# Linear-memory attention and a two-matrix feed-forward on one core: K and V in tiles of their own with fewer transfers, kept weights and first queries in larger packets, and three numbers of the schedule

## The chip, the cores and the metric

The kernel runs on one core of a Trainium2 chip. The metric is device time in microseconds (us) of one execution; lower is better. Before the change the median of three runs is 808.64 us (807.6 to 809.51).

## The reference

```python
a = phi - np.max(phi, axis=2, keepdims=True)      # phi: 8 batches, 8 heads, 576 tokens, 32 memories
a = np.exp(a)
a = a / (np.sum(a, axis=2, keepdims=True) + 1e-09)
k_m = np.einsum('bhsm,bhsd->bhmd', a, k)          # k, v, q: 8, 8, 576, 64
v_m = np.einsum('bhsm,bhsd->bhmd', a, v)
scores = scale * np.matmul(q, k_m.transpose(0, 1, 3, 2))
scores = scores - np.max(scores, axis=-1, keepdims=True)
attn = np.exp(scores)
attn = attn / (np.sum(attn, axis=-1, keepdims=True) + 1e-09)
x = np.matmul(attn, v_m)                          # then put as 4608 tokens by 512
h = x @ w_in                                      # w_in 512 x 2048
r = np.maximum(h, 0.0)
g = r * r
out = g @ w_out                                   # w_out 2048 x 512
```

The weights arrive as 64-bit floating-point numbers, and the kernel decodes them itself; the rest is 32 bits wide.

## The kernel before, in words

**Work.** Batches are handled in pairs. For each batch and each half `hh` of its heads (four heads), `memory(b, hh)` loads `phi`, K and V, takes the exponential and sums over the tokens with matmuls into the PSUM tile `pkv`: one pass for the sums of the exponential (`sums`, L465 to L471), one for K and V together (`mm`, L452). `scores(b, hh)` loads Q, transposes it on VectorE (L595), multiplies it with the K memory on TensorE (`psc`, L600) and transposes back (L604); a softmax follows. Batches 0 and 1 use `first_attention` instead, which transposes Q on TensorE (`pq`) and has its own score matmuls (`psc`, L662).

The attention output is never formed. `vw_alone` and `vw_step` multiply the V memory with a slice of `w_in` into `pvw` (L542, L562), so that `mm1(g)` goes from attention weights (`ath`, `atl`) straight to the hidden layer `h` (L766). Numbers are kept as a high and a low part, so a product is three matmuls. A step g is one batch and one block of 128 hidden units, 128 steps in all. After `h` come a relu into `r` (L770 on ScalarE or L771 on VectorE), the square's high part `gh` (L772, ScalarE), the full square (L774 or L775) and its low part `glo` (L776). `mm2(g)` adds these with `w_out` into four banks `acc` (L796, L797 from `gh`, L799 from `glo`). The 64 tokens left over beyond 512 are collected for two batches and done in `accl` (L822).

**Weights.** `decode` turns 512 KB of raw weights into a high and a low part with nine or so operations on VectorE and ScalarE, 32 times in all, ahead of the steps that use them. The decoded slices of `w_in` are written to two DRAM tensors, `w_in_hi` and `w_in_lo`, from the POOL queue (L390), and read again for each further pair of batches by `wi_again` on the SP queue (L395), two transfers of 256 KB each time.

**Order.** Nothing waits in program order as written. Each piece of work is recorded with a planned duration for each engine that can do it, what it reads and what it writes, and `Plan.order` lays all of it out by a model of the engines and the transfers; the kernel's instructions are then issued in that order. So numbers in the code that only describe durations move instructions. On the chip every engine's queue is in order, SP's queue of transfers too: a transfer that waits for a buffer holds those behind it. Buffers are tags: the tile `q` has one buffer, so Q of a batch's second half is loaded after the transposes (L595) of the first half; K and V of the next half batch are loaded after the matmuls L452 of the one before.

Of the kernel before, what the change touches and what calls it, by code (L numbers as in the profile page):

```python
# [19 lines left out]
P = 128  # L20
# [35 lines left out]
class Plan:  # L56
# [59 lines left out]
    def order(self):  # L116
# [30 lines left out]
        while len(out) < len(self.ops):  # L147
# [81 lines left out]
def tile_attention_moe(  # L229
# [54 lines left out]
    rate = {128: 100, 256: 220, 512: 288, 1024: 300, 2048: 312, 4096: 325, 4608: 325}  # L284
# [8 lines left out]
    def vec(ways, fn, r, w, **more):  # L293
        return op(ways, fn, r=r, w=w, **more)
# [27 lines left out]
    w_in_parts = []  # L322
    for x in ("hi", "lo"):
        t = dram.tile([DM, FF], F32, name=f"w_in_{x}")
        w_in_parts.append(plan.buf(f"w_in_{x}", lambda _, t=t: t))
# [3 lines left out]
    def wi_rows(x, s, hh):  # L329

        return w_in_parts[x]()[2 * hh * P:(2 * hh + 2) * P, s * SL:(s + 1) * SL].rearrange("(c p) f -> p c f", p=P)

    def decode(kind, j, h, room):

        rb, wb = (st([P, 2 * ND], U32, tag, name, 2 if tag == "KV" else 1) for tag, name in zip(room, ("raw", "work")))
# [52 lines left out]
        if kind == "wi":  # L388
            for x in (0, 1):
                dma(lambda d, x=x: d(wi_rows(x, j, h), t()[:, x].bitcast(F32)), [(2048 * P, 1024)], r=[(t, (h, x))], w=[(w_in_parts[x], (j, h))], eng="POOL", lead=True)  # L390

    def wi_again(n, s, hh):
        t = wi[n, s, 1, hh] = st([P, 2, 2, SL], F32R, "wi", f"wi{n}_{s}_{hh}", 3)
        for x in (0, 1):
            dma(lambda d, x=x: d(t()[:, x].bitcast(F32), wi_rows(x, s, hh)), [(2048 * P, 1024)], issue=440, r=[(w_in_parts[x], (s, hh))], w=[(t, (hh, x))], lead=True)  # L395
# [22 lines left out]
    def memory(b, hh, where=None):  # L418
# [550 lines left out]
```

## Time and profile before

| | |
|---|---|
| median of 3 runs | 808.64 us (807.6, 808.64, 809.51) |
| the profiled execution, its own time | 806.47 us |
| its span (first to last instruction) | 804.7 us, so 1.77 us lie around it |
| TensorE busy in the span | 774.5 us, 96% |
| VectorE, ScalarE, GpSimd busy | 561.7, 374.4, 64.7 us |
| bytes moved | 101.05 MB in 99,777 packets |

The profile names engines PE (TensorE matmuls), PEld (its weight loads), DVE (VectorE), ACT (ScalarE), POOL (GpSimd) and SP (the queue that issues most transfers). A row of a list in order of time has the start, the duration, engine, line, operation, what is written from what, and in brackets the idle time of the engine before it with what ended it. Matmuls overlap, so one that is listed with 0.39 us can be followed 0.23 us later by the next.

### The profile page before, as it was taken

How to read it: one execution, taken by the hardware profiler on the slowest of the kernel's cores; microseconds unless marked ns; L12 is line 12 of the kernel's file. 1: busy time of each engine (PE TensorE's matmuls, PEld its weight loads, DVE VectorE, ACT ScalarE, POOL GpSimd, SP SyncE). 2: the span in 40 equal slices, each digit the busy share in tenths (PEclk: the TensorE clock that was granted, in tenths of full speed). 3: DMA queues.
4: the chain of work that ended last, by engine and by line, in shares of the span. 5: the costliest groups of instructions: out<-in, count | busy, mean ns of one | idle time of the engine just before them, and what ended most of it. 6: DMA issues, size and time to landing. Idle time of an engine off the chain costs nothing.

```text
span 804.7 us, 13313 instructions
## 1 busy us (share of the span) xinstructions
PE 774.5 (96%) x4926; PEld 654.2 (81%) x4926; DVE 561.7 (70%) x1241; ACT 374.4 (47%) x871; POOL 64.7 (8%) x103
## 2 busy tenths in 40 slices
PE   4899999999999999999999999999999999999997
PEld 2677988888878888888887888788887888888885
DVE  4798867976669666966878566875779566775442
ACT  2667767865443454533343454443324345443220
POOL 4113112320101000010000100010000100000000
PEclk9999999999999999999999999999999999999999
DMA  7999865786645433321464522510524433101002
GB/s 229 278 314 285 234 176 170 217 226 178 186 118 160 121 106 105 81 50 29 128 173 122 130 95 91 138 30 25 147 63 119 128 113 99 37 7 47 1 0 66
DMA packets 99777, 101.05 MB, mean 126 GB/s; under 512 B 32320, under 2 KB 85568, under 8 KB 99712
## 3 DMA queue, kind: packets, MB, share of 16 engines
q1 hardware_dynamic: 89152, 81.42, 34.8%
q0 software_dynamic: 10464, 18.65, 8.9%
q8 instruction: 39, 0.64, 0.3%
q14 instruction: 26, 0.21, 0.1%
q10 hardware_dynamic: 96, 0.13, 0.1%
HBM read 79.17 MB, written 17.83 MB: 121 GB/s over the span
## 4 chain that ended last, share of the span: by engine, by line
PE 68%; DVE 13%; DMA 7%; issue 5%; ACT 4%; SPq 3%; POOL 1%; ACTq 0%; DVEq 0%; POOLq 0%
PE h L766 19%; PE acc L796 12%; PE acc L799 11%; PE acc L797 11%; DMA q<-in_q_dram 5%; PE accl L822 4%; DVE vw L571 3%; PE pvw L562 3%; PE pkv L452 2%; ACT vw L282 2%; ACT gh L772 1%; PE psc L600 1%; DVE qT L595 1%; DVE r L771 1%; DVE glo L776 1%
## 5 line engine op out<-in xcount | busy, mean ns | idle before, releaser
L796 PE MATMUL acc<-wo,gh 128*128 128x512 f32 x512 | 207.2, 405 | 3.9 <-ACT gh L772 3.9
L766 PE MATMUL h<-ath,vw 128*128 128x320 f32 (+1 forms) x1024 | 209.7, 299 | 0.1
L797 PE MATMUL acc<-wo,gh 128*128 128x512 f32 x512 | 201.5, 394 | 0.0
L766 PEld LDWEIGHTS h<-ath,vw 128*128 128x128 f32 x1024 | 169.0, 188 | 14.8 <-DVE r L771 0.9
L772 ACT ACTIVATE gh<-r 128x512 fp32r<-128x512 f32 x128 | 81.0, 633 | 194.1 <-DVE r L771 187.0
L799 PE MATMUL acc<-wo,glo 128*128 128x512 f32 x512 | 164.6, 406 | 0.7 <-DVE glo L776 0.5
L282 ACT CAST vw<-pvw 64x256 fp32r<-64x256 f32 (+1 forms) x224 | 84.2, 396 | 82.1 <-PE pvw L562 68.2
L796 PEld LDWEIGHTS acc<-wo,gh 128*128 128x128 f32 x512 | 96.6, 189 | 26.2 <-ACT gh L772 6.7
L797 PEld LDWEIGHTS acc<-wo,gh 128*128 128x128 f32 x512 | 96.7, 189 | 17.0
L766 PE MATMUL h<-atl,vw 128*128 128x320 f32 (+1 forms) x512 | 109.5, 295 | 0.0
L799 PEld LDWEIGHTS acc<-wo,glo 128*128 128x128 f32 x512 | 90.7, 189 | 19.2 <-DVE glo L776 5.0
L776 DVE TENSOR_TENSOR glo<-r,gh 128x512 fp32r<-128x512 f32 x128 | 87.9, 687 | 11.0 <-ACT r L774 7.3
L771 DVE TENSOR_SCALAR r<-h 128x320 f32<-128x320 f32 (+1 forms) x106 | 48.1, 456 | 68.0 <-PE h L766 64.9
L571 DVE TENSOR_TENSOR vw<-pvw,vw 64x256 fp32r<-64x256 f32 x192 | 76.9, 418 | 25.4 <-ACT vw L282 23.3
L770 ACT ACTIVATE r<-h 128x320 f32<-128x320 f32 (+1 forms) x150 | 61.1, 410 | 57.8 <-PE h L766 56.5
L766 PEld LDWEIGHTS h<-atl,vw 128*128 128x128 f32 x512 | 82.1, 189 | 0.2 <-DVE atl L694 0.2
L775 DVE TENSOR_TENSOR r<-r 128x576 f32<-128x576 f32 x59 | 44.7, 758 | 42.1 <-ACT gl L773 42.1
L822 PE MATMUL accl<-wo,gl 128*128 128x512 f32 x192 | 52.6, 395 | 0.1
L774 ACT ACTIVATE r<-r 128x576 f32<-128x576 f32 x69 | 47.4, 687 | 1.7
L822 PEld LDWEIGHTS accl<-wo,gl 128*128 128x128 f32 x192 | 35.0, 188 | 7.4 <-DVE o L282 0.5
L562 PE MATMUL pvw<-wi,VTh 128*128 128x256 f32 x192 | 37.6, 288 | 1.8 <-DVE vw L571 1.8
L562 PEld LDWEIGHTS pvw<-wi,VTh 128*128 128x128 f32 x192 | 31.2, 191 | 7.2 <-issue 3.2
(136 smaller groups left out, 855.3 us busy)
## 6 DMA issues: line engine op xcount, KB each, us to landing
wi<-w_in_hi SPq DMA_DIRECT2D x56, 256.0 KB
wi<-w_in_lo SPq DMA_DIRECT2D x56, 256.0 KB
KV<-in_k_dram SPq DMA_DIRECT2D x32, 256.0 KB
KV<-in_v_dram SPq DMA_DIRECT2D x32, 256.0 KB
raw<-in_moe_w_in_dram SPq DMA_DIRECT2D x16, 512.0 KB
raw<-in_moe_w_out_dram SPq DMA_DIRECT2D x16, 512.0 KB
q<-in_q_dram SPq DMA_DIRECT2D x24, 288.0 KB
out_dram<-o POOLq DMA_DIRECT2D x20, 256.0 KB, 7.8
```

What stands on the lines that cost most here:

```text
L282: nc.scalar.copy(o, i) if e == "ACT" else ENG[e].tensor_copy(o, i)
L562: nc.tensor.matmul(pw()[:, x * SL:(x + 1) * SL], l()[:, 2 * hh + x, :], w(r, x), start=(i == 0), stop=(i == 2))
L571: vec({"DVE": tt(SL)}, lambda e, V=V, pr=pr, src=src: nc.vector.tensor_sub(V()[pr, 1, hh, :], src(), V()[pr, 0, hh, :].bitcast(F32)), [pw, ...
L766: nc.tensor.matmul(p()[:, 0:n], V()[:, l, hh, c0:c0 + P], x()[:, hh, cs], start=(i == 0), stop=(i == 5))
L770: op({"ACT": act(n) - 40, **({} if b < 2 else {"DVE": tt(n)})}, lambda e, cs=cs, n=n, p=p: nc.scalar.activation(r()[:, cs], p()[:, 0:n], A ...
L771: else nc.vector.tensor_scalar(r()[:, cs], p()[:, 0:n], 0.0, None, ALU.max), [p], [(r, h)])
L772: op({"ACT": act(SM)}, lambda e: nc.scalar.activation(gh(), r()[:, 0:SM], AF.Square), [r], [gh])
L776: vec({"DVE": tt(SM)}, lambda e: nc.vector.tensor_sub(glo(), r()[:, 0:SM], gh().bitcast(F32)), [r, gh], [glo])
L796: nc.tensor.matmul(a(), gh()[:, c], t()[:, 0], start=f0, stop=False)
L797: nc.tensor.matmul(a(), gh()[:, c], t()[:, 1], start=False, stop=False)
L799: nc.tensor.matmul(a(), glo()[:, c], t()[:, 0], start=False, stop=f1)
L822: nc.tensor.matmul(a(), G()[:, l, :], t()[:, w], start=(ff == 0 and n == 0), stop=(ff == NFF - 1 and n == 2))
```

## The change

K and V of a half batch get a tile each (for `b` >= 2 two parts of one tile) and are loaded for four heads at once, so a `memory` has four K and V transfers where it had eight. For batches 0 and 1 the matmuls of K and of V are recorded apart, 20 with 64 columns each instead of 20 with 128. Q of the first two batches comes in one transfer for four heads with 1 KB in a row, not four with 256 bytes; this changes which token stands where, so the score matmuls of `first_attention` use a K memory spread out with zeros (`kbd`, set to zero on POOL and filled by two ScalarE copies), and the stores of these batches step over rows. The kept `w_in` is one DRAM tensor with 4 KB rows, one transfer of 512 KB each way. In the schedule, what a transfer feeds is taken to be ready 600 ns after it, loads with 4608-byte rows (Q of the later batches) move at 190 where the model had 325, and the copies and subtractions of `vw_step` take 378 and 432 where the formulas gave 260 and 326.

```diff
-                u.ready = max(u.ready, o.end + (MARGIN if "PE" in u.ways and e != "PE" else 0))
+                u.ready = max(u.ready, o.end + (600 if o.size else MARGIN if "PE" in u.ways and e != "PE" else 0))
-    rate = {128: 100, 256: 220, 512: 288, 1024: 300, 2048: 312, 4096: 325, 4608: 325}
+    rate = {128: 100, 256: 220, 512: 288, 1024: 300, 2048: 312, 4096: 325, 4608: 190}
...
         if kind == "wi":
-            for x in (0, 1):
-                dma(lambda d, x=x: d(wi_rows(x, j, h), t()[:, x].bitcast(F32)), [(2048 * P, 1024)], r=[(t, (h, x))], w=[(w_in_parts[x], (j, h))], eng="POOL", lead=True)
+            dma(lambda d: d(wi_rows(j, h), t().rearrange("p x c f -> p (x c f)").bitcast(F32)), [(4096 * P, 4096)],
+                r=[(t, (h, 0)), (t, (h, 1))], w=[(w_kept, (j, h))], eng="POOL", lead=True)
...
-        KV = []
-        for x in (0, 1):
-            t = st([P, 4 * SC * D], F32, where[x] if where else "KV", f"KV{u}_{x}", 1 if where else 2)
-            kv = lambda t=t: t().rearrange("p (i h c d) -> p i h c d", i=2, h=2, c=SC)
-            for i, src in ((0, k), (1, v)):
-                dma(lambda d, i=i, src=src, kv=kv, x=x: tokens(d, kv()[:, i], src[b, 4 * hh + 2 * x:4 * hh + 2 * x + 2]),
-                    [(2 * SM * D * 4, 1024), (2 * LEFT * D * 4, 256)], [], [(t, i)], issue=620, lead=True)
+        for i, src in ((0, k), (1, v)):
+            dma(lambda d, i=i, src=src: tokens(d, kv(i), src[b, 4 * hh:4 * hh + 4]),
+                [(4 * SM * D * 4, 1024), (4 * LEFT * D * 4, 256)], [], [KV[i]], issue=620, lead=True)
...
-        op({"PE": 1400}, mm, [A, KV[0][0], KV[1][0], pk], [pk], lead=True, lat=120)
+        if b < 2:
+            for i in (0, 1):
+                op({"PE": 800}, lambda e, i=i: mm(e, i), [A, KV[i], (pk, "sum")], [(pk, i)], lead=True, lat=120)
+        else:
+            op({"PE": 1400}, lambda e: mm(e, 0), [A, KV[0], KV[1], (pk, "sum")], [(pk, 0), (pk, 1)], lead=True, lat=120)
...
-                op({"ACT": acp(SL)}, lambda e, V=V, pr=pr, src=src: copy(e, V()[pr, 0, hh, :], src()), [pw], [(V, (hh, 0, hf))], lead=True)
+                op({"ACT": 378}, lambda e, V=V, pr=pr, src=src: copy(e, V()[pr, 0, hh, :], src()), [pw], [(V, (hh, 0, hf))], lead=True, lat=30)
...
-            for x in (0, 1):
-                for h in (2 * x, 2 * x + 1):
-                    dma(lambda d, hh=hh, Q=Q, h=h: d(Q()[:, :, h * D:(h + 1) * D], q[b, 4 * hh + h, 0:SM].rearrange("(c p) d -> p c d", p=P)),
-                        [(SM * D * 4, 256)], [], [(Q, h)], issue=550, lead=True)
+            dma(lambda d, hh=hh, Q=Q: d(Q(), q[b, 4 * hh:4 * hh + 4, 0:SM].rearrange("h (p c) d -> p h (c d)", c=NMAIN)),
+                [(4 * SM * D * 4, 1024)], [], [Q], issue=600, lead=True)
```

What the program issues differs in three places that matter below. Names carry batch, half and a running number; lines of the changed kernel are its own (L401 and L402 load like L403 and L404, L597 like L583, L785 is the relu L771, L789 the square L775, L790 is L776, L791 is L777, L585 is L571).

**SP's queue, Q of batch 2, second half.** Before, K and V of batch 4 come in eight transfers ahead of it:

```order
L403 DMA KV4_0_0_2761<-in_k_dram 128x2x256
L404 DMA KV4_0_0_2761<-in_k_dram 64x2x64
L403 DMA KV4_0_0_2761<-in_v_dram 128x2x256
L404 DMA KV4_0_0_2761<-in_v_dram 64x2x64
L403 DMA KV4_0_1_2804<-in_k_dram 128x2x256
L404 DMA KV4_0_1_2804<-in_k_dram 64x2x64
L403 DMA KV4_0_1_2804<-in_v_dram 128x2x256
L404 DMA KV4_0_1_2804<-in_v_dram 64x2x64
L403 DMA phi4_1_2764<-in_phi_dram 128x4x128
L404 DMA phi4_1_2764<-in_phi_dram 64x4x32
L583 DMA q2_1_2845<-in_q_dram 64x1152 x2
```

In the changed kernel, at the same place:

```order
L401 DMA KV4_0_2765<-in_k_dram 128x4x256
L402 DMA KV4_0_2765<-in_k_dram 64x4x64
L401 DMA KV4_0_2765<-in_v_dram 128x4x256
L402 DMA KV4_0_2765<-in_v_dram 64x4x64
L401 DMA phi4_1_2768<-in_phi_dram 128x4x128
L402 DMA phi4_1_2768<-in_phi_dram 64x4x32
L597 DMA q2_1_2819<-in_q_dram 64x1152 x2
```

Ten issues stood ahead of the Q load, six do now.

**SP's queue at the program's start, Q of batch 0.** Before, from the first raw weights (`raw`) on:

```order
L348 DMA raw_117<-in_moe_w_in_dram 128x2x512
L403 DMA KV0_1_0_119<-in_k_dram 128x2x256
L404 DMA KV0_1_0_119<-in_k_dram 64x2x64
L403 DMA KV0_1_0_119<-in_v_dram 128x2x256
L404 DMA KV0_1_0_119<-in_v_dram 64x2x64
L403 DMA KV0_1_1_169<-in_k_dram 128x2x256
L404 DMA KV0_1_1_169<-in_k_dram 64x2x64
L403 DMA KV0_1_1_169<-in_v_dram 128x2x256
L404 DMA KV0_1_1_169<-in_v_dram 64x2x64
L348 DMA raw_191<-in_moe_w_in_dram 128x2x512
L628 DMA q0_0_196<-in_q_dram 128x4x64 x4
L628 DMA q0_1_216<-in_q_dram 128x4x64 x4
```

In the changed kernel:

```order
L346 DMA raw_106<-in_moe_w_in_dram 128x2x512
L401 DMA KV0_1_1_108<-in_v_dram 128x4x256
L402 DMA KV0_1_1_108<-in_v_dram 64x4x64
L401 DMA KV0_1_0_120<-in_k_dram 128x4x256
L402 DMA KV0_1_0_120<-in_k_dram 64x4x64
L346 DMA raw_124<-in_moe_w_in_dram 128x2x512
L640 DMA q0_0_129<-in_q_dram 128x4x256
L640 DMA q0_1_154<-in_q_dram 128x4x256
```

The first raw weights are issue 13 before and 9 now; the first Q transfer is issue 23 before and 15 now, and two follow one another where eight did.

**VectorE in the middle of batch 2 (steps 36 and 37).** Before, between the relu of step 36 and that of step 37:

```order
L771 TENSOR_SCALAR r36_3331<-h36_0_3323 128x256
L775 TENSOR_TENSOR r36_3331<-r36_3331 128x576
L571 TENSOR_TENSOR vw1_0_3_3300<-pvw1_3_1_3335,vw1_0_3_3300 64x256 x2
L776 TENSOR_TENSOR glo36_3372<-r36_3331,gh36_3342 128x512
L571 TENSOR_TENSOR vw1_1_3_3304<-pvw1_3_1_3335,vw1_1_3_3304 64x256 x2
L777 TENSOR_TENSOR gl36_3357<-r36_3331,gl36_3357 128x64
L771 TENSOR_SCALAR r37_3364<-h37_0_3377 128x256
```

In the changed kernel:

```order
L785 TENSOR_SCALAR r36_3322<-h36_0_3315 128x256
L585 TENSOR_TENSOR vw1_0_3_3285<-pvw1_3_1_3324,vw1_0_3_3285 64x256 x2
L790 TENSOR_TENSOR glo36_3358<-r36_3322,gh36_3332 128x512
L791 TENSOR_TENSOR gl36_3347<-r36_3322,gl36_3347 128x64
L585 TENSOR_TENSOR vw1_1_3_3291<-pvw1_3_1_3324,vw1_1_3_3291 64x256 x2
L785 TENSOR_SCALAR r37_3356<-h37_0_3368 128x256
```

The square of step 36 (L775) has left VectorE; it stands on ScalarE. TensorE's own order at this place is the same in both: `h` of step 37, four `acc` from `glo36`, `pvw`, then `acc` from `gh37`. That group of four stands 6 times in the program before and 12 times in the changed one.

## Rows read from the trace of the kernel before

**Rows 1.** The profile's page: busy time of each engine with its share of the span, and the share of each in the chain that ended last.

```profile
PE 774.5 (96%) x4926; PEld 654.2 (81%) x4926; DVE 561.7 (70%) x1241; ACT 374.4 (47%) x871; POOL 64.7 (8%) x103
...
PE 68%; DVE 13%; DMA 7%; issue 5%; ACT 4%; SPq 3%; POOL 1%; ACTq 0%; DVEq 0%; POOLq 0%
```

**Rows 2.** Busy time of each engine by stretch of the span: the stretch, its length, busy us (and number) of PE, PEld, DVE, ACT, POOL, the granted clock, the share of the DMA engines, GB/s.

```profile
0.00:10.00 10.00, 2.08 (x50) 1.48 (x54) 2.48 (x5) 2.33 (x3) 7.31 (x15) 1.00 0.61 172
10.00:20.00 10.00, 6.94 (x88) 3.66 (x76) 6.38 (x18) 2.84 (x5) 1.14 (x2) 1.00 0.98 287
20.00:30.00 10.00, 9.40 (x105) 7.95 (x97) 4.75 (x16) 5.47 (x10) 2.39 (x4) 1.00 0.95 280
30.00:40.00 10.00, 7.09 (x37) 4.68 (x36) 10.00 (x23) 7.12 (x15) 0.00 (x0) 0.83 1.00 274
40.00:50.00 10.00, 9.82 (x82) 6.82 (x81) 9.96 (x20) 7.79 (x17) 2.17 (x3) 1.00 1.14 307
...
230.00:240.00 10.00, 8.11 (x40) 6.56 (x39) 5.62 (x11) 4.11 (x9) 0.00 (x0) 1.00 0.58 149
240.00:250.00 10.00, 10.00 (x43) 8.32 (x42) 8.45 (x19) 2.80 (x8) 0.54 (x1) 0.83 0.48 138
...
400.00:450.00 50.00, 48.38 (x304) 40.13 (x293) 38.09 (x92) 20.13 (x47) 3.11 (x6) 1.00 0.51 136
```

**Rows 3.** Who waited for whom on PE: us in total, times, longest.

```profile
PE acc L796 <- ACT gh L772: 3.9, 9, 0.7
PE psc L600 <- DVE qT L595: 3.8, 3, 1.9
```

**Rows 4.** SP's queue in order of time around 230 us: start, duration of the issue, line, transfer.

```profile
226.04 0.38 SPq L403 DMA_DIRECT2D KV<-in_k_dram  x1
...
232.44 0.60 SPq L404 DMA_DIRECT2D phi<-in_phi_dram  x1
233.14 1.20 SPq L583 DMA_DIRECT2D q<-in_q_dram  x2
```

**Rows 5.** DVE, and then PE, in order of time at the same place.

```profile
230.39 0.84 DVE L595 STREAM_TRANSPOSE qT<-q 128x640 f32<-128x640 f32 x1 [0.72 <-PE psc L600]
...
238.50 0.71 DVE L595 STREAM_TRANSPOSE qT<-q 128x512 f32<-128x512 f32 x1 [2.47 <-DMA q<-in_q_dram]
...
236.98 0.40 PE L799 MATMUL acc<-wo,glo 128*128 128x512 f32 x1
239.27 1.24 PE L600 MATMUL psc<-qT,kb 128*128 128x256 f32 x4 [1.89 <-DVE qT L595]
...
242.45 0.63 PE L796 MATMUL acc<-wo,gh 128*128 128x512 f32 x1
...
243.90 0.40 PE L796 MATMUL acc<-wo,gh 128*128 128x512 f32 x1
```

**Rows 6.** The same three queues for Q of batch 4, second half (SP, DVE, PE).

```profile
418.30 10.05 SPq L583 DMA_DIRECT2D q<-in_q_dram  x4
...
416.04 0.84 DVE L595 STREAM_TRANSPOSE qT<-q 128x640 f32<-128x640 f32 x1
...
423.80 0.71 DVE L595 STREAM_TRANSPOSE qT<-q 128x512 f32<-128x512 f32 x1 [1.69 <-DMA q<-in_q_dram]
...
424.57 1.13 PE L600 MATMUL psc<-qT,kb 128*128 128x256 f32 x4 [1.36 <-DVE qT L595]
```

**Rows 7.** All engines in order of time around step 37 of batch 2.

```profile
287.67 0.76 DVE L775 TENSOR_TENSOR r<-r 128x576 f32<-128x576 f32 x1 [1.66 <-ACT gl L773]
...
290.05 0.86 DVE L571 TENSOR_TENSOR vw<-pvw,vw 64x256 fp32r<-64x256 f32 x2
290.07 1.20 PE L799 MATMUL acc<-wo,glo 128*128 128x512 f32 x4
...
291.20 0.42 DVE L771 TENSOR_SCALAR r<-h 128x256 f32<-128x256 f32 x1
...
291.70 0.28 PE L562 MATMUL pvw<-wi,VTl 128*128 128x256 f32 x1
291.72 0.63 ACT L772 ACTIVATE gh<-r 128x512 fp32r<-128x512 f32 x1 [2.85 <-DVE r L771]
...
292.40 0.50 PE L796 MATMUL acc<-wo,gh 128*128 128x512 f32 x1 [0.42 <-ACT gh L772]
```

**Rows 8.** The start: SP's queue, then PE, in order of time.

```profile
0.80 0.45 SPq L403 DMA_DIRECT2D phi<-in_phi_dram  x1
...
14.98 7.37 SPq L628 DMA_DIRECT2D q<-in_q_dram  x8
...
8.84 0.81 PE L465 MATMUL pkv<-ones,phi 128*32 128x1 f32 x40 [1.68 <-ACT phi L443]
...
16.57 1.91 PE L376 MATMUL pd<-work,ident 128*128 128x512 f32 x2
...
18.71 0.63 PE L378 MATMUL pd<-wi,minus 128*128 128x512 f32 x1
...
25.84 0.63 PE L639 MATMUL pq<-ident,q 128*128 128x128 f32 x4 [0.59 <-DMA q<-in_q_dram]
...
41.07 0.40 PE L766 MATMUL h<-ath,vw 128*128 128x256 f32 x2
```

**Rows 9.** K and V with 128 columns at full clock, PE in order of time.

```profile
224.54 1.43 PE L452 MATMUL pkv<-KV,phi 128*32 128x128 f32 x40
```

More of the change, by code (lines that the diff above doesn't have):

```diff
@@ L321, in tile_attention_moe, with wi_rows @@
     w_out_u = w_out.bitcast(U32).rearrange("(j p) (e t) -> p j e t", p=P, t=2)
[L322 to L325, printed above, removed]
+    kept = dram.tile([NSL * 2 * P, 4 * SL], F32, name="w_in_kept")
+    w_kept = plan.buf("w_in_kept", lambda _: kept)
     wi = {}
     wo = {}
-    def wi_rows(x, s, hh):
-        return w_in_parts[x]()[2 * hh * P:(2 * hh + 2) * P, s * SL:(s + 1) * SL].rearrange("(c p) f -> p c f", p=P)
+    def wi_rows(s, hh):
+        return w_kept()[(2 * s + hh) * P:(2 * s + hh + 1) * P, :]
     def decode(kind, j, h, room):
-        rb, wb = (st([P, 2 * ND], U32, tag, name, 2 if tag == "KV" else 1) for tag, name in zip(room, ("raw", "work")))
+        rb, wb = (st([P, 2 * ND], U32, tag, name) for tag, name in zip(room, ("raw", "work")))
         if kind == "wi":
@@ L443, in memory, with mm @@
         op({"ACT": act(640)}, lambda e: nc.scalar.activation(a(), a(), AF.Exp), [A], [A], lead=True)
-        pk = pt("pa", f"pkv{u}")
+        bank = lambda name: pt("acc", name, 4) if b == 0 else pt("pa", name)
+        pk = bank(f"pkv{u}")
         rot = 2 * (b % 2)
-        def mm(e):
+        def mm(e, which):
             for c in range(SC):
@@ L637, in turn @@
                 def turn(e, x=x, Q=Q, pq=pq):
-                    for c in range(NMAIN):
-                        nc.tensor.transpose(pq()[:, c * P:(c + 1) * P], Q()[:, c, 2 * x * D:(2 * x + 2) * D], ident)
-                op({"PE": 400}, turn, [(Q, 2 * x), (Q, 2 * x + 1)], [pq], lead=True, lat=240)
-                op({"ACT": acp(SM)}, lambda e, x=x, qT=qT, pq=pq: nc.scalar.copy(qT()[:, x], pq()), [pq], [(qT, x)], lead=True)
+                    for i in range(4):
+                        nc.tensor.transpose(pq()[:, i * P:(i + 1) * P], Q()[:, 2 * x + i // 2, (i % 2) * P:(i % 2 + 1) * P], ident)
+                op({"PE": 400}, turn, [Q], [pq], lead=True, lat=240)
+                op({"ACT": acp(SM)}, lambda e, x=x, qT=qT, pq=pq: nc.scalar.copy(
+                    qT()[:, 2 * x:2 * x + 2].rearrange("p h c t -> p (h c t)"), pq()), [pq], [(qT, x)], lead=True)
             qTs.append(qT)
@@ L659, in mm @@
             def mm(e, qT=qT, kbd=kbd, pc=pc):
-                for c in range(NMAIN):
+                for s in range(4):
                     for x in (0, 1):
-                        nc.tensor.matmul(pc()[:, c * P + 64 * x:c * P + 64 * x + 64], qT()[:, pair(x), c * P:(c + 1) * P],
-                                         kbd()[:, 64 * x:64 * x + 64], start=True, stop=True)
+                        nc.tensor.matmul(pc()[:, s * P + 64 * x:s * P + 64 * x + 64], qT()[:, (s + 2 * b) % 4, x],
+                                         kbd()[:, s].rearrange("p c m -> p (c m)"), start=True, stop=True)
             op({"PE": 1780}, mm, [qT, kbd], [pc], lead=True)
             flat = lambda S_=S_: S_().rearrange("p c m -> p (c m)")
-            op({"ACT": acp(SM)}, lambda e, flat=flat, pc=pc: nc.scalar.copy(flat()[:, 0:SM], pc()), [pc], [(S_, 0)], lead=True)
+            op({"ACT": acp(SM)}, lambda e, flat=flat, pc=pc: nc.scalar.copy(
+                flat()[:, 0:SM].rearrange("p (c s m) -> p s c m", s=4, m=M), pc().rearrange("p (s c m) -> p s c m", s=4, m=M)), [pc], [(S_, 0)], lead=True)
             if hh:
@@ L850, in store @@
                 elif n == 4:
-                    rows = rows[32 * c:32 * (c + n)]
+                    rows = rows[0:SM].rearrange("(p c) e -> c p e", c=NMAIN)[c // 4]
                 else:
```

62 lines of the change are left out of this document (39 added, 23 removed).

## The prediction, written before the run

> **What bounds the kernel now.** I read the page first, then the waits of TensorE, then the busy time by stretch, and last the queues in order of time at each wait that looked removable. The page says that TensorE is busy for 96% of the span and carries 68% of the chain that ended last [rows 1]. So the time is TensorE's work, which this change leaves almost as it is, plus the time in which TensorE stands still or runs slowly. That second part is all there is to win. The busy time by stretch shows where it lies: 10 - 2.08, 10 - 6.94, 10 - 9.40 and 10 - 7.09 us, 14.5 us together, in the first 40 us, then 1.9 us at 230 to 240 us [rows 2]. The granted clock is 0.83 in two stretches, 30 to 40 and 240 to 250 us, the second right behind the idle time at 237 us.
>
> Two waits of TensorE recur later: 3.8 us for the transposed queries (`qT`), in three places, and 3.9 us for `gh`, in nine [rows 3]. The change touches both by order alone.
>
> **Q of the second half (gain 3.8 us).** At 226.04 us SP begins to issue K and V of batch 4, eight transfers, then two of `phi`, and only then, at 233.14 us, Q of batch 2 [rows 4]. The transposes that need it wait 2.47 us on VectorE and TensorE 1.89 us behind them [rows 5]. The ten issues take 233.14 - 226.04 = 7.1 us, 0.71 us each; six take 4.3 us, so SP is free at 230.3. The buffer of Q is free once the transpose that starts at 230.39 and takes 0.84 is over, at 231.2. Q can therefore go out at about 231.2, 1.9 us sooner, and from its issue to the transpose there are now 238.50 - 233.14 = 5.4 us; the transpose would start near 236.6 and TensorE could go on at 239.27 - 1.9 = 237.4, just when the matmul before it (236.98, then 0.4) is done. The order of TensorE in the changed kernel also puts more matmuls between the first and the third score matmul of this batch. At batch 4 the same arithmetic gives less: Q goes out at 418.30, and the buffer is free at 416.04 + 0.84 = 416.9, so 1.4 us can be won against a wait of 1.36 [rows 6]. The third wait is the remaining 3.8 - 1.89 - 1.36 = 0.55 us. I take all 3.8 us. The bounds: nothing, if the data and not the issue is what is late, and 3.8.
>
> The Trainium skill's page "DMA: Bandwidth & Descriptors" (section "Issuing engines are not separate DMA queues") speaks against this term: it says that the sequencer's time to start a transfer is usually small relative to the transfer itself. By that the Q load would land when it does today, and the whole sum below would be smaller by this term and the next. The trace does not agree here: the issues are 0.6 us each, and ten of them take longer than the 5.4 us from Q's issue to its use [rows 4, 5].
>
> **The clock behind that wait (gain 1.7 us).** Right behind the 1.89 us of idle time an `acc` matmul takes 0.63 us at 242.45 and the same one 0.40 at 243.90 [rows 5], and the stretch 240 to 250 has a granted clock of 0.83 [rows 2]: 10 x (1 - 0.83) = 1.7 us of TensorE's time is lost because part of it ran at the lower of the two levels (1.2 instead of 2.4 GHz). Behind the wait of 1.36 us at 424.57 [rows 6] no such fall shows: the clock is 1.00 from 400 to 450 us [rows 2]. If the wait goes, this goes. Bounds: 0 and 1.7.
>
> **`gh` in the odd steps (gain 1.9 us).** At 287.67 VectorE squares step 36, then makes `glo`, then two subtractions of `vw` (290.05, 0.86 us), then a short one, and only at 291.20 the relu of step 37, on which `gh` (291.72) and `acc` (292.40, 0.42 us idle) hang [rows 7]. In the new order VectorE no longer squares step 36 there. The 0.76 us of the square then leave a queue in which the relu was late by what `h` allowed: `h` of step 37 is done near 290.1, when the four `acc` ahead of `pvw` begin (290.07). With 0.7 us less ahead of it the relu starts at about 290.5, `gh` at 291.0, and it is ready at 291.65; TensorE ends `pvw` at 291.82 (291.70 and 0.12 to the next). So the wait would just close, and the group of matmuls in which it occurs now stands 12 times instead of 6. All nine waits are worth 3.9 us [rows 3]; because the margin is 0.2 us and there are twice as many places, I take half, 1.9. Bounds: +3.9 lost (twelve waits where there were six) and 3.9 gained.
>
> What takes the square over is ScalarE, which stands idle for 2.85 us ahead of `gh` of step 37 [rows 7]; a square that takes VectorE 0.76 us is hidden there even if it takes ScalarE twice that. Without this cover `gh` would be late by what is left over.
>
> **The start (gain 1.5 us).** SP issues 22 transfers from 0.80 to 14.98 us, 0.64 us each, and then eight of Q until 22.35; the last lands just before 25.84 [rows 8]. In the new order Q's two issues are number 15 and 16 and end at about 11 us. By their shapes the transfers up to Q's end carry 0.59 MB of `phi`, 2.36 of K and V, 1.05 of raw weights and 1.05 of Q, 5.05 MB, 18 us at 280 GB/s [rows 2]; from 2.5 us on, Q lands at about 20.5 instead of 25.8, 5 us earlier. But the first `h` (41.07) hangs on more. VectorE is busy for 10.00 and 9.96 of 10 us from 30 to 50 us, and idle for 7.5, 3.6 and 5.2 us in the three stretches before [rows 2]; only as far as that idle time is filled can the start move. And in the new order TensorE does a weight correction (`pd`) between V's and K's matmuls of the second half batch, which takes 2.8 us at that time (16.57 to 18.71 + 0.63 [rows 8]); K's memory, and with it the second score matmul, waits for it. From 5 us less up to 3 us more I take 1.5 us less, near the smaller end because VectorE is the bound there.
>
> **What costs more (0.5 us).** For batches 0 and 1 there are 40 matmuls with 64 columns in each of four half batches instead of 20 with 128. Twenty with 128 take 1.43 us at full clock [rows 9]; twenty with one column take 0.81 us at the lower one [rows 8]. So 40 with 64 columns lie between 1.43 and 2.86 us, up to 1.4 us more each, 5.7 us in all; columns halve, so they are nearer to the lower end, and two of the four half batches lie in the start, where TensorE waits anyway. I take 0.25 us for each of the other two. The zeros for `kbd` are POOL's, which is busy for 64.7 of 804.7 us [rows 1] and after the first 10 us for 1.1 of 10 [rows 2]; without that cover each would add the few tenths of one memset to the start. The second ScalarE copy lies beside VectorE's full 20 us. Fewer and larger transfers of the kept weights I cost at nothing: the DMA engines are busy for about half of the time at 230 to 250 and 400 to 450 us [rows 2], `wi` has three buffers, and if a load of it came late the next `pvw` would wait for it on TensorE by as much. The stores of the first two batches change which rows they write, and no later work waits for them.
>
> **Sum.** 806.47 - 3.8 - 1.7 - 1.9 - 1.5 + 0.5 = 798.1 us for the execution that was profiled. The median of the runs shown is 808.64, 2.2 us above that execution, so the forecast for the median is 800.3 us.
>
> **The rivals.** (a) *The data is late, not the issue.* Behind the earlier issue the same 2.06 MB (K and V 1.18, `phi` 0.29, Q 0.59) queue up, and Q arrives as now; the terms of 3.8 and 1.7 fall away. For it: Q takes 5.4 us from issue to use, long for 0.6 MB. Against it: the DMA engines are busy for 0.58 of 230 to 240 us [rows 2]. The time: 800.3 + 3.8 + 1.7 = 805.8.
> (b) *The start moves in full.* Q's 5 us come through, since VectorE's 16 us of idle time are enough to fill, and the clock fall at 30 to 40 us (0.83, another 1.7 us) goes too. For it: that fall also stands behind idle time. Against: VectorE is full. The time: 800.3 - 3.5 - 1.7 = 795.1.
> (c) *Slower: Q of batches 3, 5 and 7 comes too late.* In the new order Q of batch 3, second half, is no longer loaded far ahead but after its first half's transposes, as for batches 5 and 7. If SP is held by a kept-weight load that waits for its buffer, Q is late by that wait, and TensorE stands still and then runs at the lower clock as at 237 us: 1.9 + 1.7 = 3.6 us and more. From 2.8 us at each of the three places on it outweighs the 8.4 us above; with 4 us each the time is 800.3 + 12 = 812.3. Against it: the kept-weight load just ahead of Q there waits for a `pvw` that comes before these score matmuls.
> (d) *Nothing moves that counts.* TensorE's order is full everywhere and new waits of some tenths replace the old ones: 808.6.
>
> **How the numbers follow.** Forecast 0.62, with its own range 796 to 804.5; (b) 0.13; (a) 0.08; (d) 0.08; (c) 0.09. A measurement of this kernel can tell about 0.2% from no change, 1.6 us. Faster by more than that are the forecast, (b) and (a) but for a little: 0.82. Within it are (d) and the edge of (a): 0.09. Slower: 0.09. For 8 in 10 the range takes in (b) down to 793 and (a) and part of (d) up to 808.
>
> **What would show it.** Right: Q's second-half load is issued about 2 us after K and V's last, no wait of `psc` for `qT` over 0.3 us, a granted clock of 1.00 from 240 to 250 us; no 0.4 us of idle time before `acc` behind `pvw`; the first `h` at 39 to 40 us. Wrong: the sum of idle time after 60 us as large as now under other names; the first `h` after 42 us; TensorE idle at 320, 505 or 690 us before the third score matmul of a batch.

## The result and the profile after

The changed kernel takes 789.67 us (median; 789.19 to 790.16) against 808.32 us for the kernel before on the same chip: a ratio of 0.977, interval 0.9756 to 0.9785, 18.6 us faster. The forecast was 800.3 us with a range down to 793. The direction held and the size did not: 8.4 us were predicted and more than twice that came. The profiled execution took 789.56 us, 16.9 less than the one that the prediction's sum started from.

The page of the changed kernel, busy time and chain, as in [rows 1]:

```profile
PE 768.2 (98%) x5086; PEld 657.0 (83%) x5086; DVE 548.7 (70%) x1215; ACT 382.9 (49%) x901; POOL 50.0 (6%) x91
...
PE 94%; DVE 3%; ACT 1%; DMA 0%; issue 0%; SPq 0%; DVEq 0%; ACTq 0%
```

TensorE now carries 94% of the chain. Its busy time fell by 6.3 us although it has 160 instructions more. So the busy time before held lost time that no idle row shows; about 1.7 us of it are one stretch less at a granted clock of 0.83 (two before, one now, 10 x (1 - 0.83) each), and how waits hide in busy time is read below. The Trainium skill says in "Perfetto Trace Analysis", section "Identifying the Most-Contended Engine", that the busy share of matmuls is a poor measure of how near TensorE is to its limit, and names two others, one of them the busy share of weight loads; here that went from 81% to 83% of the span.

The stretches that answer to [rows 2]:

```profile
30.00:40.00 10.00, 8.13 (x47) 4.96 (x45) 10.00 (x22) 6.93 (x14) 0.57 (x2) 1.00 1.06 335
40.00:50.00 10.00, 7.73 (x105) 5.73 (x106) 7.24 (x16) 5.81 (x13) 0.53 (x1) 0.83 0.40 143
...
230.00:240.00 10.00, 10.00 (x56) 8.68 (x55) 7.62 (x16) 6.06 (x14) 0.00 (x0) 1.00 0.67 157
240.00:250.00 10.00, 10.00 (x50) 8.29 (x49) 9.17 (x21) 3.67 (x10) 0.54 (x1) 1.00 0.57 148
400.00:450.00 50.00, 50.00 (x302) 42.62 (x301) 39.41 (x88) 21.46 (x53) 4.25 (x7) 1.00 0.55 144
```

From 230 us on TensorE has no idle time in these stretches and no clock below 1.00. The start is not better: 40 to 50 us has 7.73 us of work where it had 9.82, and a granted clock of 0.83. Of the waits in [rows 3] the one for `qT` is gone and the one for `gh` happens once; the longest that are left, for `pmx` and `h`, lie at the start:

```profile
PE pmx L441 <- DVE mx L439: 6.4, 2, 6.0
PE h L780 <- DVE atl L708: 1.4, 1, 1.4
...
PE acc L810 <- ACT gh L786: 0.7, 1, 0.7
```

To see where the time went I took from both traces the start of the last `acc` from `glo` of a step (TensorE works through the 128 steps in the same sequence in all kernels) and compared the lengths of the stretches between, in us. The columns are kernels of the experiments below, with one execution each. That of `transfers_only` took 814.29 us, 3.5 above its median; in steps 0 to 28 it has one wait of 3.46 us for ScalarE's `vw` copy, at 146 us, and a granted clock of 0.77 from 140 to 150 us:

| stretch | before | transfers_only | loads_only | numbers_only | changed |
|---|---|---|---|---|---|
| to step 0 | 54.10 | 57.22 | 54.03 | 54.36 | 57.25 |
| steps 0 to 28 | 179.90 | 185.54 | 179.98 | 178.54 | 178.87 |
| 28 to 32 (Q of batch 2) | 36.21 | 33.51 | 31.29 | 30.26 | 30.18 |
| 32 to 64 | 183.07 | 184.47 | 183.76 | 178.87 | 179.16 |
| 64 to 80 (`vw_step`) | 86.79 | 86.34 | 86.00 | 82.59 | 82.59 |
| 80 to 96 | 98.26 | 98.14 | 96.63 | 96.34 | 96.33 |
| 96 to 127 | 150.33 | 151.06 | 150.55 | 147.17 | 147.14 |

The changed kernel loses 3.2 us at the start, and gains 1.0 by step 28, 6.0 around step 30 and 13.2 behind step 32, 17.1 in all. The two columns at the right differ only in the first row, by 2.9 us, and by 0.3 us in two others.

### The profile page after: what moved, and what is told of

The parts are those of the page before. It is cut to its first block, busy times and chain, and to the rows that moved or that the text cites. A ratio compares the mean times of both kernels' runs of the same rounds, so it can differ in the third digit from the quotient of the medians.

```text
span 787.8 us, 13443 instructions
## 1 busy us (share of the span) xinstructions
PE 768.2 (98%) x5086; PEld 657.0 (83%) x5086; DVE 548.7 (70%) x1215; ACT 382.9 (49%) x901; POOL 50.0 (6%) x91
## 4 chain that ended last, share of the span: by engine, by line
PE 94%; DVE 3%; ACT 1%; DMA 0%; issue 0%; SPq 0%; DVEq 0%; ACTq 0%
PE h L780 26%; PE acc L810 16%; PE acc L811 15%; PE acc L813 15%; PE accl L836 6%; PE pvw L576 4%; PE pkv L461 3%; PE psc L614 3%; PE pvw L556 3%; PE pd L374 1%; PE psc L675 1%; DVE mx L439 1%; PE pvw L564 0%; DMA phi<-in_phi_dram 0%; PE pd L375 0%
## 5 line engine op out<-in xcount | busy, mean ns | idle before, releaser
L780 PE MATMUL h<-ath,vw 128*128 128x320 f32 (+1 forms) x1024 | 212.1, 299 | 0.0
L780 PEld LDWEIGHTS h<-ath,vw 128*128 128x128 f32 x1024 | 171.4, 189 | 15.2 <-issue 0.4
L813 PE MATMUL acc<-wo,glo 128*128 128x512 f32 x512 | 158.1, 398 | 0.0
L784 ACT ACTIVATE r<-h 128x320 f32<-128x320 f32 (+1 forms) x161 | 66.3, 415 | 81.1 <-PE h L780 78.1
L790 DVE TENSOR_TENSOR glo<-r,gh 128x512 fp32r<-128x512 f32 x128 | 87.9, 686 | 17.1 <-ACT r L788 11.9
L585 DVE TENSOR_TENSOR vw<-pvw,vw 64x256 fp32r<-64x256 f32 x192 | 76.5, 417 | 30.3 <-ACT vw L282 29.0
L785 DVE TENSOR_SCALAR r<-h 128x256 f32<-128x256 f32 (+1 forms) x95 | 42.4, 446 | 65.8 <-PE h L780 64.9
L789 DVE TENSOR_TENSOR r<-r 128x576 f32<-128x576 f32 x59 | 44.8, 759 | 40.5 <-ACT gl L787 40.3
```

The lines of the kernel that those rows point to most:

```text
L585: vec({"DVE": 432}, lambda e, V=V, pr=pr, src=src: nc.vector.tensor_sub(V()[pr, 1, hh, :], src(), V()[pr, 0, hh, :].bitcast(F32)), [pw, (V ...
L780: nc.tensor.matmul(p()[:, 0:n], V()[:, l, hh, c0:c0 + P], x()[:, hh, cs], start=(i == 0), stop=(i == 5))
L784: op({"ACT": act(n) - 40, **({} if b < 2 else {"DVE": tt(n)})}, lambda e, cs=cs, n=n, p=p: nc.scalar.activation(r()[:, cs], p()[:, 0:n], A ...
L790: vec({"DVE": tt(SM)}, lambda e: nc.vector.tensor_sub(glo(), r()[:, 0:SM], gh().bitcast(F32)), [r, gh], [glo])
L813: nc.tensor.matmul(a(), glo()[:, c], t()[:, 0], start=False, stop=f1)
```

## Experiments

A label stands for a kernel; "numbers" are the three edits of the schedule's numbers, which change no transfer and no tile. Medians and ratios to the kernel before are given. The runs come in four sets, and the kernel before, measured in each, has medians of 807.5 to 808.6 us, so a difference of 1 us between kernels of two sets says little.

**The change in two: numbers and transfers.** `numbers_only` is the kernel before with

```diff
-                u.ready = max(u.ready, o.end + (MARGIN if "PE" in u.ways and e != "PE" else 0))
+                u.ready = max(u.ready, o.end + (600 if o.size else MARGIN if "PE" in u.ways and e != "PE" else 0))
-    ... 4608: 325}
+    ... 4608: 190}
-                op({"ACT": acp(SL)}, ... lead=True)
-                vec({"DVE": tt(SL)}, ... lead=True)
+                op({"ACT": 378}, ... lead=True, lat=30)
+                vec({"DVE": 432}, ... lead=True, lat=30)
```

and `transfers_only` is the changed kernel with these lines as before.

> The kernel before with only the schedule's numbers of the change (`vw` copies and subtractions at 378 and 432 ns with 30 ns of latency, 600 ns after a transfer, rate 190 for 4608 KB of width); all transfers and tiles as before. Theory 1: the numbers move the second half's work so that the many short waits of TensorE around `pvw`, `glo` and `gh` close, worth about 10 of the 18.6 us: 797 to 800 us, with the distance from one `acc` to the next in steps 64 to 80 as in the changed kernel. Theory 2: the gain comes from fewer SP issues and larger packets: within 2 us of before, 806 to 809 us, and the 1.89 us wait near 237 us stays in both theories.

> The changed kernel with the schedule's numbers put back to those of before (`vw` durations by the old formulas, no 600 ns after a transfer, 4608 at 325); only the tiles and transfers changed. Theory 1 (numbers bring the gain around `pvw`): 797 to 801 us, the waits near 237 us gone but the short waits of steps 64 to 80 still there. Theory 2 (transfers bring all): 789 to 792 us. Under both the start is as late as in the changed kernel, about 3 us later than before at step 0.

Measured: 786.05 us (0.9731, interval 0.9694 to 0.9767) and 810.77 us (1.0041, 1.0020 to 1.0062). Both theories fall: the numbers bring more than the whole gain, and the transfers and tiles alone lose 3.3 us (1.6 to 5.0). In the table the changed kernel is `numbers_only` plus about 3 us at the start.

**Q's wait without an earlier Q.** `loads_only` has the first two of the three edits, `lands_only` only the 600, `rate_only` only the 190.

> The kernel before with only the two numbers on loads (600 ns after a transfer, 4608 at 190). Theory A, the parts add up: all numbers gave 808 to 786 us, the `vw` durations alone about 10 of them, so the loads' numbers give the other 10 to 11 us: 796 to 799 us, with 5 to 6 us of it between steps 28 and 32 (Q of batch 2) and 2 us each between 60 and 64 and 92 and 96, and the gain within steps 64 to 80 missing. Theory B, it takes both sets together: 803 to 808 us.

> The kernel before with 600 ns after a transfer alone. If the planner's idea of when a load can be used is what puts Q and its transposes at a better place: as with both numbers on loads, 796 to 800 us, and the 1.89 us wait near 237 us gone. If the rate of 4608 is what counts: 806 to 809 us with that wait still there.

> The kernel before with 4608 at 190 alone, that is the planner takes K and V (and raw weights) to land later than it took before. If this rate is what counts: 796 to 800 us. If 600 ns after a transfer counts: 806 to 809 us.

Measured: 799.56 (0.9895, 0.9870 to 0.9921), 801.65 (0.9920, 0.9890 to 0.9951) and 802.14 us (0.9921, 0.9894 to 0.9949). Theory A comes nearest for the two together: 799.56 lies just above its 796 to 799, and steps 28 to 32 gave 4.9 us, steps 60 to 64 and 92 to 96 0.9 and 1.7. Neither case of the other two expectations came, as both kernels lie between them: either number alone does most of it (6.1 and 5.6 of 8.2 us), so neither "600" nor "190" is the cause by itself. Both tell the planner that loads land later; the rows of 4608 bytes are those of Q of the later batches, and not of K, V or the raw weights, as the expectation for `rate_only` has it. SP of `loads_only`, then VectorE and TensorE, at the place of [rows 4, 5]:

```profile
226.05 0.37 SPq L403 DMA_DIRECT2D KV<-in_k_dram  x1
...
233.73 1.20 SPq L583 DMA_DIRECT2D q<-in_q_dram  x2
...
239.10 0.71 DVE L595 STREAM_TRANSPOSE qT<-q 128x512 f32<-128x512 f32 x1 [0.37 <-DMA q<-in_q_dram]
...
237.68 0.40 PE L562 MATMUL pvw<-wi,VTh 128*128 128x256 f32 x2
...
238.38 0.39 PE L796 MATMUL acc<-wo,gh 128*128 128x512 f32 x1
...
239.77 0.39 PE L797 MATMUL acc<-wo,gh 128*128 128x512 f32 x1
240.00 1.02 PE L600 MATMUL psc<-qT,kb 128*128 128x256 f32 x4
```

K and V still come in eight transfers, Q is issued 0.6 us later than before (233.73 against 233.14) and its transpose starts 0.6 us later. TensorE does not wait, because a `pvw` group and seven `acc` now stand ahead of the score matmul (`psc`), which came right behind 236.98 before. So the wait was removed by what was put ahead of it. Earlier Q goes part of the same way: in `transfers_only`, with six issues ahead of it, the wait is still there but shorter, 0.51 us against 1.89, and the three waits for `qT` come to 1.7 us against 3.8:

```profile
237.50 1.13 SPq L597 DMA_DIRECT2D q<-in_q_dram  x2
...
244.59 1.13 PE L614 MATMUL psc<-qT,kb 128*128 128x256 f32 x4 [0.51 <-DVE qT L609]
```

The two don't add: with the numbers, the transfers win nothing there (30.26 and 30.18 us).

**The `vw` durations.** `vw_only` is the kernel before with the last edit alone, `no_vw` the changed kernel without it; `vw_dve` and `vw_act` are `loads_only` with one of its two lines.

> The kernel before with the `vw` durations alone. If they close the short waits around `pvw`: 798 to 801 us, with the gain in steps 60 to 110. If they need the other edits: 806 to 809 us.

> The changed kernel without the `vw` durations alone (600 ns after a transfer and 190 stay). If the `vw` durations close the short waits: 797 to 800 us, 8 to 10 us above the changed kernel, and all of it after 280 us. If it is the order that other edits bring about: 789 to 791 us.

> The kernel before with the two numbers on loads and, of the `vw` durations, VectorE's alone (432 ns of the engine and 30 ns until the result is seen, in place of 326 and 125; the copy on ScalarE stays at 260 and 150). Theory V: the planner filled VectorE with 4 x (418 - 326) = 0.37 us too much work at each of 48 `vw` steps, and TensorE paid 0.28 us of it each time; so this number brings most of the 13.5 us between 799.6 and 786.1: 786 to 790 us. Theory A: it is ScalarE that was overfilled (366 ns against 260): 797 to 801 us. Theory B, both are needed: 792 to 797 us.

> The same with ScalarE's `vw` copy alone at 378 ns (and 30 ns until seen), VectorE's subtraction left at 326 and 125. Theory V: 797 to 801 us. Theory A: 786 to 790 us. Theory B: 792 to 797 us.

Measured: 797.47 us (793.75 to 801.75; 0.9873, 0.9819 to 0.9927), 802.49 (0.9941, 0.9923 to 0.9959), 792.12 (0.9790, 0.9752 to 0.9828) and 791.39 (0.9784, 0.9752 to 0.9817). The edit brings 12.8 us in the changed kernel (802.49 - 789.67) and 13.5 on top of the numbers on loads (799.56 - 786.05); read from the ratios it is 13.7 and 13.2. Both are more than the 8 to 10 us expected, so that `no_vw` lies 2.5 us above its first case, which is still the nearer. Of the last two, theory B comes nearest: VectorE's number gives 7.4 of the 13.5 and ScalarE's 8.2. Each alone gives more than half and the two add to 15.6, so they overlap.

What the planner had wrong is in the rows of the kernel before, by line and form (busy, mean ns, idle):

```profile
L571 DVE TENSOR_TENSOR vw<-pvw,vw 64x256 fp32r<-64x256 f32 x192 | 76.9, 418 | 25.4 <-ACT vw L282 23.3
L282 ACT CAST vw<-pvw 64x256 fp32r<-64x256 f32 x192 | 65.6, 366 | 70.8 <-PE pvw L562 68.2 <-DVE vw L571 1.3
```

The old formulas (`tt(256)` is 60 + 1.04 x 256, `acp(256)` 55 + 0.8 x 256) gave the subtraction 326 ns and the copy 260, and then 125 and 150 ns until the result is seen. With the edit the result is seen at nearly the same time (462 for 451 ns, 408 for 410), but the engine is held for 432 and 378 ns. So the planner had put 4 x (418 - 326) = 0.37 us too much on VectorE and 4 x (366 - 260) = 0.42 us on ScalarE at each of 48 `vw_step` calls, up to 18 and 20 us. The measured 13.5 us are 0.28 us per call.

How it reaches TensorE is seen in `loads_only` (first block) against `numbers_only` at the same step, around 460 and 452 us:

```profile
456.18 0.76 DVE L775 TENSOR_TENSOR r<-r 128x576 f32<-128x576 f32 x1 [1.66 <-ACT gl L773]
456.95 0.86 DVE L571 TENSOR_TENSOR vw<-pvw,vw 64x256 fp32r<-64x256 f32 x2
...
459.71 0.43 DVE L771 TENSOR_SCALAR r<-h 128x256 f32<-128x256 f32 x1
...
460.22 0.28 PE L562 MATMUL pvw<-wi,VTl 128*128 128x256 f32 x1
460.23 0.63 ACT L772 ACTIVATE gh<-r 128x512 fp32r<-128x512 f32 x1 [2.85 <-DVE r L771]
...
460.91 0.50 PE L796 MATMUL acc<-wo,gh 128*128 128x512 f32 x1 [0.41 <-ACT gh L772]
```

```profile
449.29 0.69 ACT L774 ACTIVATE r<-r 128x576 f32<-128x576 f32 x1
...
451.99 0.42 DVE L771 TENSOR_SCALAR r<-h 128x256 f32<-128x256 f32 x1
...
452.51 0.63 ACT L772 ACTIVATE gh<-r 128x512 fp32r<-128x512 f32 x1 [1.44 <-DVE r L771]
...
452.98 0.28 PE L562 MATMUL pvw<-wi,VTl 128*128 128x256 f32 x1
...
453.19 0.50 PE L796 MATMUL acc<-wo,gh 128*128 128x512 f32 x1
```

Above, VectorE squares (L775); below, ScalarE does (L774). The relu then starts 0.99 us ahead of the last `pvw` and not 0.51, and `gh` is begun 0.47 us before that `pvw` instead of with it. From the last `pvw` to `acc` it is 0.69 us above and 0.21 below, where 0.12 us is the spacing without a wait (the prediction used it for 291.70 us). So 0.57 us are lost above, of which the bracket shows 0.41, and 0.09 below, of which it shows nothing: a matmul is listed beyond the point at which the next can start, and a short stall has no row. In steps 64 to 80 `numbers_only` is 3.4 us shorter than `loads_only`, which shows only 1.7 us of waits there (0.41, 0.42, 0.40 and 0.51). Measured as in the table, four of these 16 steps get shorter by 0.57 to 0.74 us, the one above among them, four by 0.13 to 0.20 without a row of a wait, and the other eight by 0.06 together.

**The kept weights.** `kept_too` is `numbers_only` with the kept weights' tensor and transfers of the change (512 KB with 4 KB in a row, one transfer where there were two; the 8 KB of the expectation are wrong).

> The kernel before with the schedule's numbers of the change and the kept weights stored and loaded in one transfer each with 8 KB per row; K, V and Q as before. If these transfers lie beside other work, as the prediction took it: within 1 us of the kernel with the numbers alone, 785 to 787 us. If they cost at the start: 787 to 789 us. If a larger, later load makes `pvw` wait: over 788 us, with waits of TensorE for `wi` behind 60 us.

785.10 us (784.08 to 786.38; 0.9707, 0.9674 to 0.9740). Against 786.05 (785.91 to 786.39) that is at most a small gain, as in the first case expected; no wait for `wi` appeared. It is the fastest of all here, 4.6 us under the changed kernel.

**The start.** `kv_whole` is the changed kernel with K and V of batches 0 and 1 as one piece:

```diff
-            for i in (0, 1):
-                op({"PE": 800}, lambda e, i=i: mm(e, i), [A, KV[i], (pk, "sum")], [(pk, i)], lead=True, lat=120)
+            op({"PE": 1600}, lambda e: (mm(e, 0), mm(e, 1)), [A, KV[0], KV[1], (pk, "sum")], [(pk, 0), (pk, 1)], lead=True, lat=120)
```

`kv_pa` is that with batch 0's memory in the `pa` banks of PSUM, as in the kernel before (the change had put it into those of `acc`); `kv_tiles` is `kept_too` with K and V in tiles of their own and four transfers.

> The changed kernel, but K's and V's `pkv` matmuls of batches 0 and 1 are one piece of work (1,600 ns to the planner), so that no weight correction stands between them. If that piece between them is what costs 3.4 us at the start: 786 to 787.5 us, with step 0's last `acc` 2 to 3 us earlier. If VectorE's queue sets the start whatever TensorE does: 789 to 790.5 us, the same as the changed kernel. If K's memory was gained by the split: slower, 791 to 793 us.

> The kernel before with the schedule's numbers, the kept weights in one transfer, and K and V as separate tiles in four transfers for a half batch (40 matmuls with 64 columns for batches 0 and 1, one piece of work); the queries, `kbd` and the score matmuls as before. Open is where the 4.6 us between this kernel without the K and V edit (785.1) and the changed kernel (789.7) lie; 2.5 of them are the weight correction between V's and K's matmuls. If K and V in fewer transfers cost the other 2: about 787 us. If the queries' and `kbd`'s edits cost them: 784.5 to 785.5 us. If fewer K and V transfers gain at the start: under 784 us.

> The changed kernel with K's and V's `pkv` matmuls as one piece, and with the memory's PSUM tiles of batch 0 in the `pa` banks as before instead of `acc`'s. If the banks make the start wait (the pieces of the start share fewer of them): slower than 787.2 us, 788 to 792. If it is no matter: 786.5 to 788 us. If `acc`'s banks are what costs the other 2 us: 785 us.

`kv_whole`: 787.19 us (786.95 to 787.80; 0.9741, 0.9718 to 0.9764), 2.5 us less than the changed kernel. The changed kernel's start, TensorE and then VectorE:

```profile
16.34 1.45 PE L461 MATMUL pkv<-KV,phi 128*32 128x64 f32 x40 [0.42 <-DVE rs L489]
17.71 2.07 PE L374 MATMUL pd<-work,ident 128*128 128x512 f32 x2
...
20.57 1.45 PE L461 MATMUL pkv<-KV,phi 128*32 128x64 f32 x40
...
22.09 0.35 DVE L498 TENSOR_SCALAR kvx<-pkv,rs 128x128 f32<-128x128 f32 x1 [3.55 <-PE pkv L461]
```

and `kv_whole` at the same place:

```profile
17.03 2.83 PE L461 MATMUL pkv<-KV,phi 128*32 128x64 f32 x80
...
20.20 0.34 DVE L497 TENSOR_SCALAR kvx<-pkv,rs 128x128 f32<-128x128 f32 x1
```

`pd` stands between V's and K's matmuls for 2.86 us (17.71 to 20.57), and VectorE waits 3.55 us, in a kernel whose VectorE is full from 30 to 40 us. Without it K's part is ready 1.9 us sooner.

How much of this reaches TensorE is seen at the first `h`. The changed kernel:

```profile
42.94 0.49 PE L780 MATMUL h<-atl,vw 128*128 128x256 f32 x1 [1.42 <-DVE atl L708]
...
43.65 1.91 PE L374 MATMUL pd<-work,ident 128*128 128x512 f32 x2
...
46.21 0.58 PE L780 MATMUL h<-ath,vw 128*128 128x320 f32 x2
```

and `kv_whole`, with the busy times of that stretch:

```profile
42.49 0.39 PE L779 MATMUL h<-atl,vw 128*128 128x256 f32 x1 [0.68 <-DVE atl L707]
...
42.95 1.02 PE L374 MATMUL pd<-work,ident 128*128 128x512 f32 x2
...
44.27 0.46 PE L779 MATMUL h<-ath,vw 128*128 128x320 f32 x2
...
40.00:50.00 10.00, 8.82 (x153) 6.36 (x151) 8.04 (x20) 7.01 (x16) 0.73 (x2) 1.00 0.52 179
```

The weight correction at this place begins 0.7 us later in the changed kernel (43.65 against 42.95), and to the next `h` it takes 2.56 us instead of 1.32. The granted clock is 0.83 from 40 to 50 us there, behind the idle time ahead of `h`, and 1.00 in `kv_whole`. So of the 2.1 us by which `kv_whole` ends step 0 sooner (55.11 against 57.25), more than half is the lower clock. It is not one bad execution: the mean granted clock is 0.996 or 0.997 in all five executions of the changed kernel and 1.000 in all four of `kv_whole`.

`kv_tiles`: 789.80 us, but spread from 787.21 to 793.04 (0.9782, 0.9752 to 0.9811); `kv_pa`: 786.89 us (786.35 to 792.25; 0.9759, 0.9728 to 0.9789), so in the median the banks are no matter. The spread goes with the clock: the four executions of `kv_tiles`, 793.04, 791.15, 788.45 and 787.21 us, have mean granted clocks of 0.991, 0.992, 0.999 and 1.000. The longest is the profiled one, and has a granted clock under 1.00 at four of the first six stretches:

```profile
20.00:30.00 10.00, 9.01 (x156) 7.23 (x155) 4.19 (x10) 4.69 (x8) 1.68 (x3) 0.83 1.00 295
30.00:40.00 10.00, 7.92 (x52) 6.03 (x51) 9.31 (x24) 7.33 (x15) 0.00 (x0) 0.89 0.99 276
40.00:50.00 10.00, 9.22 (x47) 6.70 (x47) 9.96 (x20) 7.51 (x17) 0.77 (x1) 0.94 0.82 244
50.00:60.00 10.00, 8.78 (x144) 6.46 (x144) 8.44 (x21) 5.18 (x11) 0.98 (x2) 0.74 0.70 222
```

So the K and V edit costs 2 us or more on top of `kept_too` (785.10) also without the `pd` between, even in the two executions at nearly full clock (787.21 and 788.45); the queries' edit is not what costs the rest, since `kv_whole` has it and takes 787.19. Which part of the K and V edit it is stays open, and so does what makes the clock fall in some executions and not in others.

**More durations from the trace.** `all_times` is `numbers_only` with all formulas of VectorE raised by 95 ns and of ScalarE by 115, and as much less until seen.

> The kernel before with the schedule's numbers of the change, and in the same sense the formulas for all other operations of VectorE and ScalarE raised to what the trace shows (95 ns more of VectorE, 115 ns more of ScalarE each, and as much less until the result is seen). If too short durations are what lets the planner overfill an engine everywhere, there is still something to win, mostly in the first 60 us: 780 to 785 us. If TensorE is full already behind 60 us and the start hangs on VectorE's work as such: 785 to 788 us. If other numbers were right together only by luck, up to 795 us.

786.16 us (785.48 to 787.02; 0.9720, 0.9688 to 0.9752): no gain. Step 0 came 2.8 us sooner and was paid back by step 12. What was put right here was not small. `glo`, for one, was planned at 60 + 1.04 x 512 = 592 ns, and in the trace before it takes 687:

```profile
L776 DVE TENSOR_TENSOR glo<-r,gh 128x512 fp32r<-128x512 f32 x128 | 87.9, 687 | 11.0 <-ACT r L774 7.3 <-PE acc L799 0.2
```

That is 12 us over 128 steps, and it was worth nothing. So it is not shown that a wrong duration costs time wherever it stands; it did for the `vw` pair.

## Why the prediction fell short, step by step

**Q of the second half: waits right, step and size wrong.** The waits for `qT` (3.8 us) are gone, and Q goes out when its buffer is free, as forecast, at 231.35 us where I had 231.2. SP, VectorE and TensorE of the changed kernel:

```profile
231.35 1.14 SPq L597 DMA_DIRECT2D q<-in_q_dram  x2
...
230.48 0.84 DVE L609 STREAM_TRANSPOSE qT<-q 128x640 f32<-128x640 f32 x1 [1.40 <-PE psc L614]
...
238.02 0.71 DVE L609 STREAM_TRANSPOSE qT<-q 128x512 f32<-128x512 f32 x1
...
239.10 1.02 PE L614 MATMUL psc<-qT,kb 128*128 128x256 f32 x4
```

But the gain was put down to fewer issues, and they are neither needed nor enough: `loads_only` loses the wait with Q issued later, `numbers_only` with ten issues ahead of Q takes 30.26 us for steps 28 to 32 where the changed kernel takes 30.18, and `transfers_only` keeps 0.51 us. The sentence that more matmuls stand ahead of the third score matmul was written down as an aside; by itself it was enough. The Trainium skill's "DMA: Bandwidth & Descriptors", section "Issuing engines are not separate DMA queues", would have the issue time small beside the transfer. That the wait falls from 1.89 to 0.51 us in `transfers_only` speaks against that for this load, but sizes and order differ there too, and no run has fewer issues alone; in the changed kernel the point decides nothing.

**The clock: right.** 1.00 from 240 to 250 us. Together with the `qT` terms, 3.6 us were predicted for steps 28 to 32 (1.89 + 1.7), 1.36 for 60 to 64 and 0.55 for 92 to 96, 5.5 in all. These stretches gave 6.0, 2.1 and 2.0 us, and with the loads' numbers alone 4.9, 0.9 and 1.7. So the two terms were too small by 2 us or more.

**`gh` in the odd steps: mechanism right, size off by seven times.** This is the term that put the forecast wrong. It was 1.9 us, and the edit that takes the square from VectorE is worth 12.8 to 13.5, in more places than the odd steps. Three steps failed. The sum took the idle rows (3.9 us) as all there was to win, while a stall is 0.16 us longer than its bracket (0.57 for 0.41) and short ones have none. It halved even that, for a margin. And it never looked at what the planner had wrong, though 48 x 0.37 and 48 x 0.42 us could be read from the trace before and the formulas. That they are a bound and no forecast is seen in `all_times`, but a bound of 18 to 20 us would have put the range's lower end well under 793.

**The start: wrong sign.** It was 1.5 us gained, and 3.2 were lost to step 0. The working named `pd` between V's and K's matmuls with up to 3 us and then took the other end, for Q that lands sooner. Q did come sooner (the issues end at 13.3 us) and won nothing; `pd`, with the fall of the clock that goes with it, cost 2.1 us to step 0 and 2.5 in the median, which `kv_whole` shows. The low clock that [rows 2] have at 30 to 40 us did not go but moved to 40 to 50 us. The remaining loss, about 1 us, belongs to the part of the K and V edit that stays open. The sign that I gave for this, a first `h` after 42 us, did not appear (40.92 us), since `h` then waits again for `atl`, 1.42 us. The mark should have been step 0's end.

**Costs and rivals.** The 64-column matmuls: right, K and V of a half batch take 1.73 us at full clock in the changed kernel where they took 1.43 [rows 9], 0.30 against the 0.25 taken:

```profile
67.45 1.73 PE L461 MATMUL pkv<-KV,phi 128*32 128x64 f32 x80
```

The working's other bound, twenty matmuls with one column at "the lower" clock, is not a reading of the rows: [rows 2] give 1.00 for that stretch. Kept weights at nothing: right within a microsecond. Rival (b) came nearest in time, for the wrong reason. Rival (c), Q late at batches 3, 5 and 7, did not occur: there is no wait for `qT`.

## What to carry to other kernels

Where a planner orders the work, a wrong duration can be a cost on its own: multiply (duration in the trace minus duration in the plan) by the number of times the operation occurs, engine by engine, and take it as the upper end of what the edit may bring. Here it was 18 to 20 us for 13 measured, and 12 us and more for nothing in `all_times`, so only a run tells. Tell apart how long an engine is held from when its result is seen. Take the worth of a stall from start to start of the matmuls, or from the length of a step, since idle time in rows leaves out what the listed end of the matmul before covers. When one edit moves transfers and another the plan, split them first: here the part that looked like the change cost time.

## What the runs showed of the hardware

Matmuls that wait show part of the wait as busy time: from `pvw` to `acc` 0.57 us were lost in `loads_only` where the bracket shows 0.41. Over the whole span 5086 instructions took 768.2 us where 4926 took 774.5; about 1.7 us of that difference are the clock. A copy of 64x256 from PSUM on ScalarE takes 366 ns and a subtraction of that shape on VectorE 418 ns, in the mean of 192 each, and two such subtractions in a row 0.86 us. Executions of one program differ by up to 8 us, and in the widest spreads the longest ones have the lowest mean granted clock: `kv_tiles` 787.2 us at 1.000 to 793.0 at 0.991, `vw_only` 793.75 at 0.996 to 801.75 at 0.988, while `numbers_only` stays within 785.9 to 786.4 at 0.996 to 1.000. Where in the execution the clock is lost is known only for the one that was profiled; in `kv_tiles` it is lost in the four stretches shown above.
